# Batch 0's x in 1 KB rows of four tokens, loaded ahead of the weights, with the hand-written order redealt

## The chip, the cores and the metric

The kernel runs on one core of a Trainium2 chip. The core has a matrix engine (TensorE, PE in the profile, with its weight loads listed apart as PEld), a vector engine (VectorE, DVE), a scalar engine (ScalarE, ACT), a general engine (GpSimd, POOL) and a queue engine (SyncE, SP) that mostly issues DMA transfers. ACT can issue DMA transfers too. The metric is the device time of one execution in microseconds (us), the median of several runs.

## The reference

Two stages follow each other. The first reads between tokens and states for each batch and head; the second is a feed-forward network with SwiGLU over all tokens and states.

```
B, H, S, Ns, D = (8, 8, 512, 32, 64)
scores = x @ state.T / sqrt(D);   a  = softmax(scores, over states)
xread  = a @ state                                   # (B, H, 512, 64)
scores2 = state @ x.T / sqrt(D);  a2 = softmax(scores2, over tokens)
sread  = a2 @ x                                      # (B, H, 32, 64)
x = concat([xread, sread], axis=2) -> (8 * 544, 512) # heads side by side
xn  = x / sqrt(mean(x * x) + 1e-6) * rms_g
g   = xn @ w_gate                                    # 512 -> 1536
out = (g * sigmoid(g) * (xn @ w_val)) @ w_out        # 1536 -> 512
```

All arithmetic is float32. The three weight matrices come as float64 in memory and are decoded on the chip.

## The kernel before

**Work and stages.** The 4352 rows are handled as eight batches of 512 tokens, and the 256 states together as a ninth batch. The weights come in 18 pieces of 1 MB of raw float64, gate, val and out for each of six pairs `mp` of 128-column blocks. Four raw buffers exist (`RAW_AHEAD`), so the load of piece k+4 is issued when piece k is decoded. Decoding a piece takes three ACT steps (`exponents`, L223: L237, L239, L242) and four DVE steps (`values`, L246: L263, L266, L270, L275). Only piece 0 (gate of mp 0) is handled in two halves, as two DMAs of 512 KB and two sets of steps. Batch 0 is computed with plain matrix products while the pieces are decoded: `own_weights` (L602) multiplies states with weights (matmuls L615, ACT copies L627), `hidden` (L647) has the matmuls L658, the ACT silu L664 and the DVE product L668, and `project_as_ready` (L858) has the matmuls L865. Batches 1 to 7 use schemes with seven products instead of eight: `hidden_seven` (L752, matmuls L762, ACT copies L814, DVE sums L825 and L838) and `project_twice` (L1034, matmuls L1065, ACT copies L1075, POOL sums L1091, DVE sums L1105, L1115 and L1124).

**The reads.** `tokens_read(b)` (L428) calls `scores` (L305). There, for batches 0 and 1, the states are transposed on PE (L310) and copied to `stT` by DVE (L313); batch 0 also forms products of the states with themselves (L321, `gram` L325). x is transposed by PE in 16 blocks of 128x128 (L333), in four groups through a PSUM tile that ACT copies to `xT` (L335). The score matmuls (L360) give two full tiles of 128x512, one for the even heads and one for the odd. For batch 0, ACT copies both to `sS` (L370), and PE transposes them back so that tokens lie in the partitions (L374, into the PSUM pool named `pv`). Then comes the softmax over states on DVE and ACT: maximum L439, subtraction L441, exponential L443, sum L451, reciprocal L454, product L456. For batch 0 the result is transposed on PE (L464) and copied to `aT_s` by ACT (L467), the squares are summed (L477, L480, L391, L396), GpSimd takes the power −1/2 (L292), four transpositions lay it along the rows (L299), and DVE multiplies it in (L500). The first L658 needs L500. For later batches the tokens' read itself is a matmul (L486), which waits for DVE's transposition L459. `states_read(b)` (L504) takes the softmax over tokens from `sS` (maximum L513, exponential L520); from batch 2 on, the exponentials go to DRAM and back with another layout (store L541, four loads L545, issued by ACT), then come the matmuls L556, the DVE scaling L567 and a transposition L571.

**How x is loaded.** For batches from 2 on, `load_x` (L128) lays token 4p+c in partition p at place c: one DMA of 1 MB, in which each partition and head gets four neighbouring tokens, 1 KB in one piece. For batches 0 and 1, token 128c+p lies in partition p: four DMAs of 256 KB, each in pieces of 256 B (one token of one head). For batch 0 two of these are issued by ACT and two by SP. SP's loads at the start stand in this order: first half of piece 0, the four DMAs of the states of batch 0 (L126), SP's part of x, second half of piece 0, piece 1, `rms_g`, pieces 2 and 3, states and x of batch 1.

```
    halves = load_parts(0)
    next(halves, None)
    load_state(0)
    load_x(0, nc.scalar, nc.scalar, nc.sync, nc.sync)
    for _ in halves:
        pass
    load_piece(1)
```

**What sets the order.** Each part of the work is a Python generator, a stream with a letter. Strings written by hand name the stream whose next step is emitted, and this order is what each engine's queue gets: an engine runs its own queue in order and waits where another engine's result is missing. `ORDER` deals the start and batch 0 (letters: `a` and `s` the token and state reads of batch 0, `A` and `S` those of batch 1, `e` exponents, `d` values, `v` own weights, `h`, `t`, `u` the three parts of `hidden`, `p`, `c` the projection, `w`, `k` preparations for batch 1, and `z` `keep_awake` at L1192, one 128x256 matmul (L1197) on the identity that nothing reads). `FIRST` deals batch 1 together with the reads of batch 2, `PERIOD` batches 2 to 6, `LAST` batch 7, and `STATES` the ninth. In these, `h`, `t`, `u` are the products, silu and sums of `hidden_seven`, `p`, `c`, `k` those of `project_twice`, `a` and `s` the reads of the next batch, `q` quarter sums of weights, `f`, `g`, `l` fetches and loads that SP issues, and `o` stores.

**Buffers in PSUM** around the change: pool `aps` ("at") has two tiles, `vps` ("pv") two, `fx` two, `fy` and `fz` one each, and each is one bank of 128x512 float32.

Of the kernel before, what the change touches and what calls it, by code (L numbers as in the profile page):

```python
# [8 lines left out]
F32 = mybir.dt.float32  # L9
# [8 lines left out]
P = 128  # L18
# [1 line left out]
W_BUFS = 3  # L20

ORDER = (
    "ddzzzzzzzzzezzzeezaaaaaaaaaaaaddaezddaseaaazzaeaaazzdaaaazdeezzzazzaaaazeeaaaadd"
    "aaadaaeAdadsdeezezAdavaaAvAAAAvhehteeAeAdddduhhppdAddtdeeedvvvudeeedphhdtheeddtA"
    "ddddeupdAAAdhAdedeeuedppvpsdAvvddAedhhpetudeeeddhtsAAdhudpAeppdddeAAeedddvAdsvvA"
    "eedphhtuseessseedddeeAhtsdhesppsdvdupdvvdhheeAddAdAtsshtpAudApAedpdhededdveuAApA"
    "AAvvheAdAtSAASSeSSdphSddShAtASuShAkuSSwwpwwkcpSScpSkkckpkcwkkkkkwwwwk"
)

PERIOD = (  # L30
# [4 lines left out]
)  # L35

FIRST = (
    "vhththhhthfhhuuuhtttuqqqqaxxaaauhthhhvquuhuxqxxaavtuhhththhfaxthhhqqquuuuxxtuhut"
    "hthhthhuaakaavfuuxhtuuhutthqqfhhutxxuqqqqqqhauthuuxhhaautthaaasshtuuhuuthuGhskuk"
    "GuGukkppqqpppqpppugqqpkkkklkppqpppkcpcqgaakppgqqkskaakaaaaqqppkkpppkppkkpkpkpkpa"  # L40
    "cosaaaacgpapgaskkkkkkaosaapppppgcppppcaappaskkakkapppkpapkappaakpookkoosaassfsww"
    "xssswxlscxxcoxofxg"
)
LAST = (
    "vxhhffththhtuhhhavuttuuhhtfuhhgxxthhhuuuxxtuthuhtthuhuxhutuvxxxvhthhutkxghhtuhut"
# [11 lines left out]
def kernel(  # L57
# [61 lines left out]
    x_sb = {}  # L119
# [6 lines left out]
            nc.sync.dma_start(out=rows[b][Ns * j:Ns * j + Ns], in_=src)  # L126

    def load_x(b, *queues):  # L128
        if b > 1:
            x_sb[b] = one.tile([P, H, NC, D], F32, name="x_b")  # L130
            nc.sync.dma_start(out=x_sb[b].rearrange("p h c d -> p h (c d)"),
                              in_=x[b].rearrange("h (p c) d -> p h (c d)", c=NC))
            return
        x_sb[b] = (one if b else x_0).tile([P, NC, H * D], F32, name="x_b")
        for c in range(NC):
            (queues or (nc.sync,))[c % max(1, len(queues))].dma_start(
                out=x_sb[b][:, c].rearrange("p (h d) -> p h d", h=H),
                in_=x[b, :, P * c:P * c + P, :].rearrange("h p d -> p h d"))

# [165 lines left out]
    def scores(b, packed, soft):  # L305

        xb = x_sb[b]
        stT = one.tile([P, 4, Ns], F32, name="stT")
        tp = aps.tile([P, 4, Ns], F32, name="at")
        TE.transpose(out=tp.rearrange("p j n -> p (j n)"),  # L310
                     in_=packed.rearrange("p e d -> p (e d)"), identity=ident)
        yield
        VE.tensor_copy(stT, tp)  # L313
        yield "step"
# [12 lines left out]

        if b < 2:
            xT = one.tile([P, 4, NC, P], F32, name="xT", tag="xT")
            for c in range(NC):  # L330
                tp = aps.tile([P, 4, P], F32, name="at")
                for j in range(4):
                    TE.transpose(out=tp[:, j, :], in_=xb[:, c, P * j:P * j + P], identity=ident)  # L333
# [23 lines left out]
        sp = [aps.tile([P, S], F32, name="at") for e in range(2)]  # L357
        for j in range(4):
            for e in range(2):
                TE.matmul(out=sp[e][Ns * j:Ns * j + Ns, :], lhsT=stT[D * e:D * e + D, j, :],  # L360
                          rhs=xT[D * e:D * e + D, j],
                          start=True, stop=True)
        yield


        sS = read[b] = (one if b else x_0).tile([P, 2, NC, P], F32, name="sS")
        eS = one.tile([P, 2, S // Ns, Ns], F32, name="eS", tag="eS")
        soft.update(st=stT, e=eS, raw=[eS[:, e] for e in range(2)])
        for e in range(2) if b == 0 else ():
            SE.copy(sS[:, e].rearrange("p c t -> p (c t)"), sp[e])  # L370
            yield
            tp = vps.tile([P, NC, P], F32, name="pv")
            for c in range(NC):
                TE.transpose(out=tp[:, c, :], in_=sS[:, e, c, :], identity=ident)  # L374
# [53 lines left out]
    def tokens_read(b):  # L428
# [21 lines left out]
        for e in range(2):  # L450
            VE.reduce_sum(out=z1[:, e], in_=eS[:, e], axis=AXX)  # L451
            yield
            VE.tensor_scalar(z1[:, e], z1[:, e], 1e-9, None, op0=ALU.add)
            VE.reciprocal(z1[:, e], z1[:, e])  # L454
            yield
            VE.tensor_tensor(out=eS[:, e], in0=eS[:, e], in1=along(z1, e), op=ALU.mult)  # L456
            yield
            if b:
                VE.transpose(out=aT_s[b][:, e], in_=eS[:, e].rearrange("p k n -> p (k n)"))  # L459
                yield "step"  # L460
                continue
            tp = aps.tile([P, NC, P], F32, name="at")
            for c in range(NC):
                TE.transpose(out=tp[:, c, :], identity=ident,  # L464
                             in_=eS[:, e, 4 * c:4 * c + 4].rearrange("p j n -> p (j n)"))
            yield
            SE.copy(aT_s[b][:, e], tp.rearrange("p c t -> p (c t)"))  # L467
            yield "step"


# [33 lines left out]
    def states_read(b):  # L504
# [47 lines left out]
        for e in range(2):  # L552
            for c in range(NC):
                for j in range(4):
                    h = 2 * j + e
                    TE.matmul(out=rp[Ns * j:Ns * j + Ns, e, :],  # L556
                              lhsT=(e2T[:, j, e, c, :] if b > 1 else
                                    flat[:, e, c, Ns * j:Ns * j + Ns]),
                              rhs=(xb[:, h, c, :] if b > 1 else xb[:, c, D * h:D * h + D]),
                              start=(c == 0), stop=(c == NC - 1))  # L560
        if b == 1:
            load_state(2)
# [650 lines left out]

    parts_0, banks_0 = {}, []
    halves = load_parts(0)
    next(halves, None)
    load_state(0)
    load_x(0, nc.scalar, nc.scalar, nc.sync, nc.sync)
    for _ in halves:
        pass  # L1220
    load_piece(1)
# [79 lines left out]
```

## Time and profile before

| | us |
|---|---|
| median of 3 runs (lowest, highest) | 760.69 (760.42, 761.26) |
| the profiled execution | 759.33 |
| its span, from first to last instruction | 757.5 |
| PE busy in the span | 743.8 (98%) |
| DVE busy | 599.3 (79%) |
| ACT busy | 350.1 (46%) |
| POOL busy | 295.2 (39%) |
| first DVE step of batch 0's softmax (L439) | 16.34 |
| first matmul of batch 0's FFN (L658) | 33.82 |

The profile describes one execution. Its times count from the start of the span, and line numbers are those of the kernel before; the changed kernel has other line numbers for the same statements. A group row names a line, an engine, an operation and its tiles, then its count, busy time and mean length, and what the engine waited for ahead of it. A row of waits gives the total, the number and the longest of the waits of one line for another. The chain of work that ended last is followed back from the end, at each step to what released it. Matmul starts follow each other faster than the length of one row says, since matmuls overlap.

### The profile page before, as it was taken

What the parts mean: (1) busy time and instruction counts of PE and PEld (TensorE: products, weight loads), DVE (VectorE), ACT (ScalarE), POOL (GpSimd) and SP (SyncE); (2) the same over time, 40 slices, a digit from 0 to 9 for tenths busy, and PEclk for the clock granted to TensorE, in tenths of its full rate; (3) what the DMA queues carried; (4) which work ended last, traced back from release to release, by engine and by line L of the source; (5) the groups of instructions that cost most, each with busy time, mean ns of one, the idle gap of its engine ahead of it and who ended that gap; (6) DMA issues with size and microseconds to landing.
All of it is one profiled execution on the core that took longest, in us unless ns stands there. A gap on an engine that the chain in (4) does not pass through costs nothing.

```text
span 757.5 us, 14370 instructions
## 1 busy us (share of the span) xinstructions
PE 743.8 (98%) x5618; PEld 592.5 (78%) x5618; DVE 599.3 (79%) x998; ACT 350.1 (46%) x546; POOL 295.2 (39%) x379
## 2 busy tenths in 40 slices
PE   8899999999899999999999999999999999999998
PEld 6534434678777898879877997789788987899997
DVE  3999996779957897689948994799579965787961
ACT  4889965544235522653255425543455236411220
POOL 3000003892584326542474129312843266323600
PEclk9999999999999999999999999999999999999999
DMA  9887855695576276825784377617661765132311
GB/s 283 234 296 249 315 185 184 243 306 168 188 238 229 45 272 215 292 58 191 248 279 118 143 258 239 195 58 303 217 225 30 302 206 214 55 100 111 139 56 29
DMA packets 61891, 146.17 MB, mean 193 GB/s; under 512 B 15744, under 2 KB 32640, under 8 KB 54912
## 3 DMA queue, kind: packets, MB, share of 16 engines
q1 hardware_dynamic: 48704, 125.78, 47.6%
q10 hardware_dynamic: 13120, 19.47, 9.0%
q8 instruction: 45, 0.74, 0.4%
q14 instruction: 22, 0.18, 0.1%
HBM read 116.46 MB, written 28.77 MB: 192 GB/s over the span
## 4 chain that ended last, share of the span: by engine, by line
PE 91%; DVE 7%; issue 1%; ACT 1%; POOL 0%; DVEq 0%; POOLq 0%
PE f L762 37%; PE f L1065 28%; PE f L865 6%; PE pv L658 6%; PE at L615 3%; PE pv L615 3%; PE f L928 2%; PE f L1197 1%; PE at L556 1%; PE at L360 1%; PE at L486 1%; DVE hb L1124 1%; PE at L299 0%; DVE hb L838 0%; DVE eS L456 0%
## 5 line engine op out<-in xcount | busy, mean ns | idle before, releaser
L762 PE MATMUL f<-aT_s,v 128*128 128x256 f32 x504 | 119.6, 382 | 0.0
L762 PEld LDWEIGHTS f<-aT_s,v 128*128 128x128 f32 x504 | 94.5, 190 | 24.8 <-issue 8.4
L1091 POOL TENSOR_TENSOR kept<-kept 128x256 f32<-128x256 f32 x28 | 23.1, 824 | 174.9 <-DVE kept L1105 173.8
L825 DVE TENSOR_TENSOR g<-g,f 128x512 f32<-128x512 f32 x84 | 57.3, 686 | 39.4 <-PE f L762 35.4
L1075 ACT COPY kept<-f 128x512 f32<-128x512 f32 (+1 forms) x56 | 29.6, 532 | 124.8 <-PE f L1065 83.1
L762 PE MATMUL f<-aT_t,vs 128*128 128x256 f32 x336 | 87.1, 383 | 0.0
L1065 PE MATMUL f<-w,h 128*128 128x128 f32 x588 | 74.6, 276 | 1.0 <-DVE h L1115 1.0
L762 PEld LDWEIGHTS f<-aT_t,vs 128*128 128x128 f32 x336 | 62.5, 190 | 15.3 <-POOL vs L642 4.2
L1065 PEld LDWEIGHTS f<-w,h 128*128 128x128 f32 x588 | 69.6, 192 | 5.5 <-issue 4.1
L816 ACT ACTIVATE hb<-g 128x1024 f32<-128x1024 f32 x42 | 44.4, 1057 | 56.6 <-DVE g L825 56.5
L642 POOL TENSOR_TENSOR vs<-v 128x256 f32<-128x256 f32 x42 | 31.4, 748 | 79.5 <-ACT v L627 79.5
L292 POOL TENSOR_TENSOR ri<-ss,mhalf 128x4 f32<-128x4 f32 x8 | 10.7, 1341 | 117.4 <-DVE ss L396 107.5
L814 ACT COPY g<-f 128x512 f32<-128x512 f32 x42 | 24.6, 586 | 45.0 <-PE f L762 45.0
L762 PE MATMUL f<-aT_t,v 128*128 128x256 f32 x168 | 43.5, 381 | 1.6 <-DVE c L825 1.6
L865 PE MATMUL f<-wo,hb 128*128 128x512 f32 x96 | 44.8, 603 | 0.0
L658 PE MATMUL pv<-aT_s,v 128*128 128x512 f32 x96 | 43.9, 595 | 0.1
L762 PE MATMUL f<-aT_s,vs 128*128 128x256 f32 x168 | 43.6, 382 | 0.0
L838 DVE TENSOR_TENSOR hb<-hb,c 128x512 f32<-128x512 f32 (+1 forms) x48 | 36.7, 764 | 8.0 <-ACT hb L816 7.2
L838 DVE TENSOR_TENSOR hb<-hb,f 128x512 f32<-128x512 f32 (+1 forms) x48 | 31.0, 646 | 15.0 <-PE f L762 14.8
L1065 PE MATMUL f<-wo,h 128*128 128x128 f32 x336 | 42.2, 275 | 0.0
L1065 PE MATMUL f<-wo,hb 128*128 128x128 f32 x336 | 42.1, 275 | 0.0
L825 DVE TENSOR_TENSOR c<-c,f 128x512 f32<-128x512 f32 (+1 forms) x48 | 31.2, 651 | 12.6 <-PE f L762 12.5
(206 smaller groups left out, 1681.4 us busy)
## 6 DMA issues: line engine op xcount, KB each, us to landing
w_m<-w_d SPq DMA_DIRECT2D x48, 1024.0 KB, 6.0
w<-t_d SPq DMA_DIRECT2D x49, 576.0 KB, 5.3
out_dram<-kept SPq DMA_DIRECT2D x56, 128.0 KB, 1.8
raw<-in_moe_w_val_dram SPq DMA_DIRECT2D x6, 1024.0 KB, 5.8
raw<-in_moe_w_out_dram SPq DMA_DIRECT2D x6, 1024.0 KB, 8.5
w_d<-w_m SPq DMA_DIRECT2D x6, 1024.0 KB, 4.9
x_b<-in_x_dram SPq DMA_DIRECT2D x6, 1024.0 KB, 7.6
x_d<-xB ACTq DMA_DIRECT2D x6, 1024.0 KB, 4.2
```

The costliest lines, as they stand in the source:

```text
L615: TE.matmul(out=pv[e][Ns * j:Ns * j + Ns, :], lhsT=stT_g[b][D * e:D * e + D, j, :], rhs=w[D * e:D * e + D, j].rearrange("p m k f -> p (m k ...
L642: GE.tensor_tensor(out=vs[:, 0], in0=a21, in1=a22, op=ALU.add)
L658: TE.matmul(out=to[0], lhsT=lhs(i, k), rhs=r, start=(i == 0), stop=(i == len(rhs) - 1))
L762: TE.matmul(out=ps[:, i, 0:half], lhsT=l[:, i, :], rhs=r, start=(start and i == 0 and k == 0), stop=(k == len(lhs) - 1), skip_group_check= ...
L814: SE.copy(gates(q)[1], q["x"][:, :, 0:half])
L816: SE.activation(out=hb[:, 2 * mp:2 * mp + 2, 0:n].rearrange("p m (c t) -> p m c t", c=2), in_=q["g"][:, :, :, 0:half], func=ACTF.Silu if s ...
L825: VE.tensor_tensor(out=to, in0=to, in1=q[ps][:, :, 0:half], op=ALU.add)
L838: VE.tensor_tensor(out=part, in0=part, in1=val, op=ALU.mult)
L865: TE.matmul(out=banks[r], lhsT=hb[:, m, P * r:P * r + P], rhs=wo[:, m, :], start=(m == 0), stop=(m == NM - 1))
L1065: TE.matmul(out=to[half][:, slot, :], lhsT=lhs[:, k, :], rhs=rhs[:, k, :], start=(fresh and n in (0, 4) and k == 0), stop=(k == QM - 1), s ...
L1075: SE.copy(k[:, 4 * i:4 * i + 4 - i], banks[name][i])
L1091: GE.tensor_tensor(out=k[:, 1:3], in0=k[:, 0:1].to_broadcast([P, 2, QD]), in1=k[:, 1:3], op=ALU.add)
```

## The change

- `load_x` gives batch 0 the layout of the later batches, token 4p+c in partition p. It is loaded by two DMAs of 512 KB in 1 KB pieces: heads 0 to 3 on ACT's queue, heads 4 to 7 on SP's.
- The states and x of batch 0 are issued ahead of both halves of piece 0.
- In `scores` for batch 0, each of the 16 transpositions takes two places (c, c+1) of one head, so that a transposed block holds one token place in the lower 64 partitions and the next in the upper 64. For this, the states are needed on both halves for every head: DVE copies the two heads of a pair in exchanged order to `swapped`, PE transposes this as well, and DVE copies both results to `both` (128x256).
- The score matmuls of batch 0 become 16 of 256 columns into four half tiles (two "at", two "pv"), ACT's copies to `sS` become four of 256 columns, and the transpositions back go to a tile of `fx`.
- The copy to `aT_s` puts the tokens back into their natural order, and the state read of batch 0 takes x by head and place.
- `ORDER` and `FIRST` are dealt anew. Four keep-awake matmuls stand ahead of the first real one on PE where there were thirteen rows of it before (26 matmuls of the record). Behind L500 on DVE stands the third step (L270) of piece 2, which stood ahead of it. In batch 1, PE's L486 stands later and its L556 and L571 earlier; `PERIOD`, `LAST` and `STATES` are as they were.

```diff
     def load_x(b, *queues):
+        if b == 0:
+            x_sb[b] = x_0.tile([P, H, NC, D], F32, name="x_b")
+            n = H // len(queues)
+            for k, queue in enumerate(queues):
+                heads = slice(n * k, n * k + n)
+                queue.dma_start(out=x_sb[b][:, heads].rearrange("p h c d -> p h (c d)"),
+                                in_=x[b, heads].rearrange("h (p c) d -> p h (c d)", c=NC))
+            return
...
     def scores(b, packed, soft):
...
+        if b == 0:
+            swapped = x_0.tile([P, 2, D], F32, name="swapped")
+            for e in range(2):
+                VE.tensor_copy(swapped[:, e], packed[:, 1 - e])
+            yield
+            both = x_0.tile([P, 2, 4, Ns], F32, name="both")
+            tp = aps.tile([P, 2, 4, Ns], F32, name="at")
+            for k, rows_ in enumerate((packed, swapped)):
+                TE.transpose(out=tp[:, k].rearrange("p j n -> p (j n)"),
+                             in_=rows_.rearrange("p e d -> p (e d)"), identity=ident)
+            yield
+            VE.tensor_copy(both, tp)
+            stT = both[:, 0]
+            yield "step"
...
+        if b == 0:
+            xT = one.tile([P, 4, 4, P], F32, name="xT", tag="xT")
+            for j in range(4):
+                tp = aps.tile([P, 4, P], F32, name="at")
+                for k in range(4):
+                    TE.transpose(out=tp[:, k, :], identity=ident,
+                                 in_=xb[:, 2 * j + k // 2, 2 * (k % 2):2 * (k % 2) + 2].rearrange("p c d -> p (c d)"))
+                yield
+                SE.copy(xT[:, j], tp)
+                yield "step"
...
+        if b == 0:
+            halves = [[pool.tile([P, 2 * P], F32, name=name) for e in range(2)]
+                      for pool, name in ((aps, "at"), (vps, "pv"))]
             for e in range(2):
-                TE.matmul(out=sp[e][Ns * j:Ns * j + Ns, :], lhsT=stT[D * e:D * e + D, j, :],
-                          rhs=xT[D * e:D * e + D, j],
-                          start=True, stop=True)
+                for j in range(4):
+                    for i in range(2):
+                        here = slice(D * i, D * i + D)
+                        TE.matmul(out=halves[i][e][Ns * j:Ns * j + Ns, :], lhsT=both[here, (e + i) % 2, j, :],
+                                  rhs=xT[here, j, 2 * e:2 * e + 2], start=True, stop=True)
...
         for e in range(2) if b == 0 else ():
-            SE.copy(sS[:, e].rearrange("p c t -> p (c t)"), sp[e])
-            yield
-            tp = vps.tile([P, NC, P], F32, name="pv")
+            for i in range(2):
+                SE.copy(sS[:, e, i::2], halves[i][e].rearrange("p (k t) -> p k t", k=2))
+            yield
+            tp = fx.tile([P, NC, P], F32, name="f")
...
-            SE.copy(aT_s[b][:, e], tp.rearrange("p c t -> p (c t)"))
+            SE.copy(aT_s[b][:, e].rearrange("p (t c) -> p t c", c=NC), tp.rearrange("p c t -> p t c"))
...
-                              rhs=(xb[:, h, c, :] if b > 1 else xb[:, c, D * h:D * h + D]),
+                              rhs=(xb[:, h, c, :] if b != 1 else xb[:, c, D * h:D * h + D]),
...
     halves = load_parts(0)
+    load_state(0)
+    load_x(0, nc.scalar, nc.sync)
     next(halves, None)
-    load_state(0)
-    load_x(0, nc.scalar, nc.scalar, nc.sync, nc.sync)
     for _ in halves:
         pass
     load_piece(1)
```

The two strings, cut (each letter one step):

```diff
 ORDER = (
-    "ddzzzzzzzzzezzzeezaaaaaaaaaaaaddaezddaseaaazzaeaaazzdaaaazdeezzzazzaaaazeeaaaadd"
...
+    "zzzzaaaaaaaaaaaaaaddeaaesaaaaedeazzzzzazdaaaaeedazzzzzedeaaaazzdadeezzaaaaddaadA"
+    "eeeaAadvvAvaaadeesdAAahthAAhddddehtupeeddduAAAdsdpedepveddpvvdddedeedhthAhhuddAe"
...
 FIRST = (
-    "vhththhhthfhhuuuhtttuqqqqaxxaaauhthhhvquuhuxqxxaavtuhhththhfaxthhhqqquuuuxxtuhut"
-    "hthhthhuaakaavfuuxhtuuhutthqqfhhutxxuqqqqqqhauthuuxhhaautthaaasshtuuhuuthuGhskuk"
...
+    "vxhhthhthhthuxuufththaaaaaqfhhqthahtqqquuuuxavvhuhhxxtuthuhthtuhuhuaqhvfxxxtuqqqx"
+    "tqhqqqqhutkqqhqtaahauhuGGhutuhhhutGuuhtthhhxxuuxtqqquaaauaahhhthagthhthsuuuuuuhp"
...
```

More of the change, by code (lines that the diff above doesn't have):

```diff
@@ L22 @@
 ORDER = (
-    "ddzzzzzzzzzezzzeezaaaaaaaaaaaaddaezddaseaaazzaeaaazzdaaaazdeezzzazzaaaazeeaaaadd"
[L24 to L27, printed above, removed]
+    "zzzzaaaaaaaaaaaaaaddeaaesaaaaedeazzzzzazdaaaaeedazzzzzedeaaaazzdadeezzaaaaddaadA"
+    "eeeaAadvvAvaaadeesdAAahthAAhddddehtupeeddduAAAdsdpedepveddpvvdddedeedhthAhhuddAe"
+    "edppedAAeeAtddveeupvvhhheddtddAepeeedtAAdhsuddpsdudAddedeedppeevpvvhAAddAdAedsht"
+    "uddedsseeAsedshhdtuppvevvphhApdAedteeeeAdeAdshduepAdtAdAAsdApAAddddehueevvAASSAv"
+    "pShSSAAAptddSSSSdSdhhAuhkkAtuwSwskSSkkkwpcSwpcpcskkpcwwkkkwwkw"
 )
@@ L37 @@
 FIRST = (
-    "vhththhhthfhhuuuhtttuqqqqaxxaaauhthhhvquuhuxqxxaavtuhhththhfaxthhhqqquuuuxxtuhut"
-    "hthhthhuaakaavfuuxhtuuhutthqqfhhutxxuqqqqqqhauthuuxhhaautthaaasshtuuhuuthuGhskuk"
-    "GuGukkppqqpppqpppugqqpkkkklkppqpppkcpcqgaakppgqqkskaakaaaaqqppkkpppkppkkpkpkpkpa"
-    "cosaaaacgpapgaskkkkkkaosaapppppgcppppcaappaskkakkapppkpapkappaakpookkoosaassfsww"
-    "xssswxlscxxcoxofxg"
+    "vxhthhthhthuxuufththaaaaaqfhhqthahtqqquuuuxavvhuhhxxtuthuhthtuhuhuaqhvfxxxtuqqqx"
+    "tqhqqqqhutkqqhqtaahauhuGGhutuhhhutGuuhtthhhxxuuxtqqquaaauaahhhthagthhthsuuuuuuhp"
+    "ppkpptukupuqqqqkkppukkkkkppaakkkggkcacppppppppcappppssaaakplqapkkkkkpkkkppppaaak"
+    "ccaasapppssakscfqaaaapqkkappkkkakppppakkosasqksappppskssgglsaoooapspppakkkaooafw"
+    "wxsxxpgcpcowxoxfxg"
 )
@@ L133, in load_x @@
             return
-        x_sb[b] = (one if b else x_0).tile([P, NC, H * D], F32, name="x_b")
+        x_sb[b] = one.tile([P, NC, H * D], F32, name="x_b")
         for c in range(NC):
-            (queues or (nc.sync,))[c % max(1, len(queues))].dma_start(
+            nc.sync.dma_start(
                 out=x_sb[b][:, c].rearrange("p (h d) -> p h d", h=H),
@@ L307, in scores @@
         xb = x_sb[b]
[L308 to L311, printed above, removed]
-        yield
-        VE.tensor_copy(stT, tp)
-        yield "step"
+        if b == 0:
[12 more added lines that the diff above has]
+            yield "step"
+        else:
+            stT = one.tile([P, 4, Ns], F32, name="stT")
+            tp = aps.tile([P, 4, Ns], F32, name="at")
+            TE.transpose(out=tp.rearrange("p j n -> p (j n)"),
+                         in_=packed.rearrange("p e d -> p (e d)"), identity=ident)
+            yield
+            VE.tensor_copy(stT, tp)
+            yield "step"
         if b == 0:
@@ L326, in scores @@
             yield "step"
-        if b < 2:
+        if b == 0:
[7 more added lines that the diff above has]
+                SE.copy(xT[:, j], tp)
+                yield "step"
+        elif b == 1:
             xT = one.tile([P, 4, NC, P], F32, name="xT", tag="xT")
@@ L354, in scores @@
             xT = xT.rearrange("p g j r -> p j g r")
-        sp = [aps.tile([P, S], F32, name="at") for e in range(2)]
-        for j in range(4):
+        if b == 0:
+            halves = [[pool.tile([P, 2 * P], F32, name=name) for e in range(2)]
+                      for pool, name in ((aps, "at"), (vps, "pv"))]
             for e in range(2):
-                TE.matmul(out=sp[e][Ns * j:Ns * j + Ns, :], lhsT=stT[D * e:D * e + D, j, :],
-                          rhs=xT[D * e:D * e + D, j],
-                          start=True, stop=True)
+                for j in range(4):
[3 more added lines that the diff above has]
+                                  rhs=xT[here, j, 2 * e:2 * e + 2], start=True, stop=True)
+        else:
+            sp = [aps.tile([P, S], F32, name="at") for e in range(2)]
+            for j in range(4):
+                for e in range(2):
+                    TE.matmul(out=sp[e][Ns * j:Ns * j + Ns, :], lhsT=stT[D * e:D * e + D, j, :],
+                              rhs=xT[D * e:D * e + D, j],
+                              start=True, stop=True)
         yield
```

## The prediction

> **What bounds the kernel now.** I read the page first. TensorE (PE) is busy 98% of the span and carries 91% of the chain that ended last; VectorE (DVE) has the next 7%.
>
> ```profile
> PE 743.8 (98%) x5618; PEld 592.5 (78%) x5618; DVE 599.3 (79%) x998; ACT 350.1 (46%) x546; POOL 295.2 (39%) x379
> PE 91%; DVE 7%; issue 1%; ACT 1%; POOL 0%; DVEq 0%; POOLq 0%
> ```
>
> So time can be won only where PE isn't doing work that the result needs: in the start, and in its waits. Second view, the table by stretches (busy time of PE, PE weight loads, DVE, ACT, POOL; then clock, DMA share, GB/s). The cuts are mine: 33.82 is the first L658, where PE starts the FFN of batch 0; 134.37 is about where batch 1 starts.
>
> ```profile
> 0.00:30.27 30.27, 25.16 (x152) 17.75 (x152) 18.44 (x34) 18.18 (x24) 6.44 (x28) 1.00 0.96 250
> 33.82:134.37 100.55, 100.55 (x515) 42.97 (x515) 92.19 (x120) 80.21 (x101) 7.50 (x9) 1.00 0.71 249
> 134.37:757.50 623.13, 614.90 (x4921) 529.85 (x4920) 485.16 (x841) 248.39 (x418) 280.57 (x342) 1.00 0.53 181
> ```
>
> From 33.82 to 134.37 PE never idles, though DVE is 92% busy beside it. The 25.16 us of PE in the start are mostly keep-awake matmuls (L1197), which compute nothing. Third view, the chain in order of time (start, length, what):
>
> ```profile
> 1.46 8.50 PE f L1197 x26
> 9.96 0.12 PE at L310
> ...
> 10.75 0.60 PE at L333 x4
> ...
> 13.83 1.20 PE at L360 x16
> ...
> 16.34 0.70 DVE m L439
> ...
> 30.70 1.13 DVE raw L266
> ...
> 33.17 0.61 DVE aT_s L500
> 33.77 0.04 issue
> 33.82 0.70 PE pv L658
> ```
>
> Until 9.8 nothing real has run on PE. Then come transposition, scores and softmax; from 16.34 to 33.77 the chain is DVE alone, without a gap that counts: softmax of batch 0 mixed with the decoding of three and a half weight pieces. So the start has two limits: when the state and x land, and then the sum of DVE's work. Fourth view, the same table for two short stretches: while the 2 KB pieces of the first half of gate move, and while x moves in 256 B pieces.
>
> ```profile
> 3.20:4.00 0.80, 0.80 (x3) 0.62 (x3) 0.00 (x0) 0.00 (x0) 0.80 (x5) 1.00 1.09 383
> 6.00:8.00 2.00, 2.00 (x9) 1.69 (x8) 0.21 (x1) 1.17 (x2) 0.32 (x1) 1.00 1.35 211
> ```
>
> Last column: 383 GB/s against 211. Fifth view, PE's waits from 134 to 230, which is batch 1 (total, times, longest):
>
> ```profile
> PE f L762 <- DVE c L825: 1.6, 1, 1.6
> PE at L486 <- DVE aT_s L459: 1.0, 1, 1.0
> PE f L1065 <- DVE h L1115: 1.0, 1, 1.0
> PE at L571 <- DVE sr L567: 0.7, 1, 0.7
> ```
>
> That is 4.3 us, all that FIRST can win. The rows of L545 in that stretch say when the exponentials of batch 2's state read come back from DRAM:
>
> ```profile
> DMA to landing us min/median/max: 5.3/7.4/7.5
> ```
>
> [...] the 128x256 keep-awake matmuls take 634 ns until about 6 us and 379 after.
>
> **The change, part by part.**
>
> *Landing.* Before: first half of gate (512 KB) at 4.96, rows and x behind it, rows usable at about 9.5. After: rows (64 KB) and x (1 MB) lead, gate follows. Bytes start to flow at about 2 us. At 383 GB/s the 1.06 MB are in by 4.8, at 211 by 7.0. Pieces of 1 KB are nowhere in this trace; [...] the rows' 256 B pieces share the engines, so I take 300: x complete at about 5.6 to 6.3, rows at 4.75, first half of gate 1.4 us later (7.7; bounds 6.3 and 8.4).
>
> *To the first L439.* Two DVE copies (128x64), two transpositions instead of one, one 128x256 copy instead of 128x128 (0.30 us, so about 0.45): the gram matmuls at about 6.15, x's transpositions from 6.6. Their 16 with four copies took 10.75 to 13.83, 3.1 us; the same again, so score matmuls at 9.7. From there to L439 it was 16.34 − 13.83 = 2.5: now 16 matmuls of 256 columns for 8 of 512 (nothing to +0.2), and ACT's four copies of 256 columns for two of 512 (about 0.35 against 0.58 each, +0.13), while the four early transpositions no longer wait for a "pv" bank. So L439 at 12.3. Only 4 keep-awake matmuls stand ahead instead of 13, then PE waits for the rows: if it is cold in the transpositions (0.17 us apart, 634/379 times that is 0.28), 16 x 0.11 = 1.8 more, of which the ACT copies (4 x 0.585) hide some. I take 12.65, bounds 12.3 and 14.1.
>
> *DVE from L439 to L658.* Before: L439 at 16.34, L500 at 33.08: 16.74. The decoding of the first half of gate was done ahead of L439 (DVE waited 5.0 for that landing and 3.9 for L310); now its last two steps (L270 and L275, 0.60 each) and the first two of the second half (0.40 and 0.60) come behind: +2.2. The L270 of the third piece (1.13) is dealt behind L500. Sum 17.8, less a 0.28 issue gap that has no reason to recur, 17.5; bounds 17.5 and 18.1, since L270 now waits for ACT's third step (about 13.8 to 14.5), and the reciprocal root on POOL (1.40, then L299) has only 2.3 us of DVE work over it instead of 3.6, against 2.6 that the path needs. I take 17.85. L658 follows L500's start by 0.74: 12.65 + 17.85 + 0.74 = 31.25, against 33.82: **2.6 us won**, from 1.0 (14.1 and 18.1) to 3.3.
>
> *33.8 to 134.* Four x transpositions of batch 1 that stood ahead of L658 stand behind it: 4 x 0.11 = +0.44 on a full PE. DVE has 1.13 more to do here: 92.2 becomes 93.3 beside 101. The pieces decoded are due at L615; queue against queue, each is done 0.3 to 1 us ahead of it. That cover is thin; gone, the excess is paid once, at most about 1. I take nothing. Start, net: **−2.2**.
>
> *FIRST.* PE's read of batch 2 (L486) stands 1.34 us later against DVE's L459 only 0.5 later: wait 1.0 to about 0.1. L571 stands further behind L567: 0.7 to nothing. One L513 less ahead of L825: 1.6 to about 0.7. L1115 slightly better (−0.3). Sum −2.8. Against it: L556 stands 5.6 us of PE work earlier, while its slack after the last L545 landing (217.0) was 0.6 (it began at 217.63). The loads are issued earlier too: I put their landing at 211 to 213, against PE's arrival at about 210.2, so with the semaphore a new wait of 1 to 3, taken 2.1; behind it stands PE's whole queue. Net **−0.7**, from −1.8 to +0.2. SP's fetches move among themselves with weights a period ahead, and POOL's L1091 sums only interleave: POOL has 174.9 us of idle ahead of them, cost nothing; if a bank's store were late it would show as a wait for L1091.
>
> *The rest.* The permuted read of the aT_s copy: 0 to +0.6 each of two, hidden by DVE's decoding between. PERIOD, LAST and STATES are unchanged, 0.
>
> Sum: −2.2 − 0.7 = −2.9. The profiled execution took 759.33 (span 757.5 and 1.83 around it): 756.4. The median shown is 760.69, 1.36 more; the same distance gives **757.7**.
>
> **The rivals**, on the median's scale.
> - More: PE is warm, x lands by 5, L556 finds its data. −3.3 + 0.4 − 1.8 = −4.7: **756.0**. The keep-awake row argues against a warm PE.
> - Eaten: x lands at 7.0 and PE is cold: L439 at 14.1 gives −1.0 + 0.44 = −0.6; with FIRST at −0.2, **759.9**. For it: both transfers share the same engines, and DVE, not landing, sets 17 of the 31 us.
> - Slower: L556. If its loads land when they did, at 217.0, PE waits until 217.2 with the 5.6 us of matmuls that used to fill this time now behind it: every other gain upstream is absorbed, and batch 1 loses 217.2 + 5.6 − 217.63 − 0.7 = 4.5. With the start's −2.2 that is +2.3: **763.0**. It decides from a loss of 3.7 on, i.e. if the loads come less than 0.8 us earlier than before. For it: landings of 7.4 us there against a median of 3.4 over all batches. Against: the new order moves the store and loads forward on ACT too.
> - The change doesn't do what it says, because DVE alone sets L658: excluded in part, since L439 itself moves; it is the "eaten" case.
>
> **Chances.** About 0.2%, 1.5 us, is what a measurement of this kernel can tell from no change. Forecast (756.0 to 759.2) 0.58; more 0.07; eaten 0.20; slower 0.15. Faster is the first two, 0.65; same 0.20; slower 0.15. The range leaves out the slower case and a little of "more": 755.3 to 760.8.
>
> **What would show it.** First L439 between 12 and 14 and first L658 near 31.2; x's packets at 300 GB/s or more; no wait of PE in the 100 us after L658; in batch 1 no wait at L486 or L571, and one at L556 of 1 to 3. Wrong if L658 comes after 32.5, if L615 waits for DVE's w_m, or if L556's wait exceeds 3.

## The result: no difference that can be measured

The changed kernel takes 760.96 us (median of 21 runs, 757.65 to 764.07) beside 760.39 for the kernel before (21 runs, 759.11 to 761.63): a ratio of 1.0006, 95% interval [0.9995, 1.0017]. The forecast was 757.7. Its runs spread over 6.4 us where those of before spread over 2.5, and they go with the clock that the throttle granted to TensorE, averaged over the run (1.000 is full speed): at 0.998 the two runs took 757.65 and 758.30, at 0.993 the eight runs took 762.0 in the median. A straight line through the 21 runs loses 0.67 us for each 0.001 of clock (correlation −0.75) and, drawn on beyond the runs, reaches 757.4 at a clock of 1.000. An estimate for comparison: 0.001 of a span of 758 us is 0.76 us of full-speed work, so most of the clock that is lost goes with a longer run.

The profiled execution took 760.29 (span 758.5). First the two lines of its page on engines and on the chain that ended last:

```profile
PE 745.1 (98%) x5619; PEld 592.8 (78%) x5619; DVE 599.4 (79%) x1000; ACT 349.8 (46%) x548; POOL 294.9 (39%) x379
PE 87%; DVE 6%; ACT 2%; DMA 2%; issue 1%; POOL 1%; SPq 0%; ACTq 0%; DVEq 0%
```

PE has 1.3 us more of busy time, though fewer keep-awake matmuls run (38 in the record, 54 before); and DMA has 2% and POOL 1% of the chain, where POOL had 0% before and DMA had no part. The table by stretches, cut at the first L702 (L658 before) and at the first matmul of batch 1:

```profile
0.00:32.88 32.88, 28.52 (x181) 19.18 (x182) 20.73 (x40) 20.88 (x30) 6.36 (x28) 0.91 0.88 268
32.88:134.66 101.78, 101.61 (x519) 43.56 (x519) 96.47 (x123) 80.39 (x102) 9.22 (x9) 0.99 0.69 245
134.66:758.50 623.84, 614.97 (x4928) 530.06 (x4920) 482.17 (x838) 248.55 (x418) 279.35 (x342) 1.00 0.53 180
```

Before, batch 1 began at 134.30. So the start became 0.94 shorter (forecast 2.6), the next stretch 1.30 longer (forecast 0.44), the rest 0.64 longer (forecast 0.7 shorter). In the rest, batch 1 took 0.3 less, batch 4 took 0.7 more, and the end, from the last long run of matmuls on, took 0.3 more. The third number from the end, the clock, is 0.91 in the start; before it was 1.00. Two views show where. The chain in order of time (start, length, what):

```profile
5.52 0.83 PE at L324 x2
...
7.21 2.85 PE at L356 x12
...
13.27 0.62 DVE m L483
...
26.74 1.49 PE f L435 x8
28.23 1.89 PE f L659 x16
30.11 1.04 PE at L366 x4
31.16 0.85 PE pv L307 x4
32.01 0.85 PE at L366 x4
...
32.88 3.37 PE pv L702 x6
```

and the stretches around its lower half (third number from the end: clock):

```profile
24.00:26.00 2.00, 1.76 (x19) 0.80 (x15) 1.97 (x3) 1.97 (x3) 0.00 (x0) 1.00 1.00 362
26.00:28.00 2.00, 1.74 (x13) 1.65 (x12) 2.00 (x4) 0.55 (x1) 0.00 (x0) 0.79 0.27 96
28.00:30.00 2.00, 2.00 (x18) 0.36 (x17) 1.75 (x5) 1.18 (x1) 1.40 (x1) 0.50 0.66 265
30.00:32.00 2.00, 2.00 (x17) 1.96 (x10) 0.75 (x1) 1.80 (x3) 0.00 (x0) 0.50 1.04 266
32.00:34.00 2.00, 1.98 (x7) 1.09 (x6) 1.95 (x3) 1.95 (x4) 0.00 (x0) 0.50 0.91 367
34.00:36.00 2.00, 2.00 (x6) 0.89 (x5) 1.97 (x3) 1.85 (x3) 0.00 (x0) 1.00 0.39 158
```

From about 27 to 34 PE has half its clock; such a stretch is called a dip below. Before, DVE carried the chain from 16.3 to 33.8; now it loses it at 26.7 to a PE whose matmuls take about twice as long: L659's sixteen 1.89 us instead of 1.02, a group of four transpositions 0.85 to 1.04 instead of about 0.5. What goes ahead in the trace is a stretch of 5 us (23.1 to 28.2) with narrow matmuls, L521 on 32 rows and L435 with one column, and a single transposition of 128x128. The last keep-awake matmuls end at 22.2. The clock falls at 27.18 and stays low for 6.83 us; in the 2.00 us ahead of the fall PE is busy for 1.74.

In batch 1, PE's waits from 134 to 230 (total, times, longest):

```profile
PE at L600 <- DMA e<-e_d: 1.5, 1, 1.5
PE f L806 <- ACT g L853: 1.2, 2, 0.8
PE f L1109 <- DVE h L1159: 0.9, 1, 0.9
PE f L806 <- DVE c L869: 0.8, 1, 0.8
PE f L1109 <- DVE h L1161: 0.4, 1, 0.4
```

The waits at the tokens' read and at the last transposition are gone and the one for L825 is halved, as forecast; L600 (L556 before) waits for its loads, as forecast, and two new small waits appeared. In sum 4.8 us instead of 4.3. (Not every wait is time lost: batch 1 as a whole still took 0.3 less.)

A third loss, 0.7 us, lies in batch 4, whose order is unchanged. The first of these rows, from the profile after, and the second, from that before, give the time that the four loads of transposed x took from issue to landing there:

```profile
DMA to landing us min/median/max: 3.3/5.0/6.0
```

```profile
DMA to landing us min/median/max: 3.4/4.7/5.3
```

The slowest of the four takes 0.7 longer after a like issue time, and the score matmuls of that batch (L403, L360 before) take 1.85 us instead of 1.17:

```profile
411.94 1.85 PE L403 MATMUL at<-xG,stT 64*32 64x512 f32 x16
```

```profile
411.88 1.17 PE L360 MATMUL at<-xG,stT 64*32 64x512 f32 x16
```

Between 404 and 412, after has one transfer more, of instructions; before has only the second of these rows there:

```profile
q8 instruction: 1, 0.02, 1.0%
q14 instruction: 1, 0.01, 0.2%
```

### The profile page after: what moved, and what is told of

Read it like the earlier page. It is cut to its first block, busy times and chain, and to the rows that moved or that the text cites. A ratio compares the mean times of both kernels' runs of the same rounds, so it can differ in the third digit from the quotient of the medians.

```text
span 758.5 us, 14372 instructions
## 1 busy us (share of the span) xinstructions
PE 745.1 (98%) x5619; PEld 592.8 (78%) x5619; DVE 599.4 (79%) x1000; ACT 349.8 (46%) x548; POOL 294.9 (39%) x379
## 4 chain that ended last, share of the span: by engine, by line
PE 87%; DVE 6%; ACT 2%; DMA 2%; issue 1%; POOL 1%; SPq 0%; ACTq 0%; DVEq 0%
PE f L806 38%; PE f L1109 26%; PE pv L702 5%; PE f L909 4%; PE at L659 3%; PE pv L659 2%; PE f L972 2%; PE at L600 1%; PE at L403 1%; PE at L530 1%; DMA e<-e_d 1%; DMA out_dram<-kept 1%; DVE hb L1168 0%; DVE hb L882 0%; ACT ex L247 0%
## 5 line engine op out<-in xcount | busy, mean ns | idle before, releaser
L1135 POOL TENSOR_TENSOR kept<-kept 128x256 f32<-128x256 f32 x28 | 23.1, 825 | 176.1 <-DVE kept L1149 174.9
L702 PE MATMUL pv<-aT_s,v 128*128 128x512 f32 x96 | 44.6, 603 | 0.2 <-ACT v L671 0.2
L869 DVE TENSOR_TENSOR c<-c,f 128x512 f32<-128x512 f32 (+1 forms) x48 | 31.3, 652 | 13.7 <-PE f L806 13.7
```

Of the source, the lines that this page charges most:

```text
L702: TE.matmul(out=to[0], lhsT=lhs(i, k), rhs=r, start=(i == 0), stop=(i == len(rhs) - 1))
L869: VE.tensor_tensor(out=to, in0=to, in1=q[ps][:, :, 0:half], op=ALU.add)
L1135: GE.tensor_tensor(out=k[:, 1:3], in0=k[:, 0:1].to_broadcast([P, 2, QD]), in1=k[:, 1:3], op=ALU.add)
```

## The experiments

Theory 1 when they began: the start's gain is real, and is lost to the clock dip at 27. Rival 2: it is lost in batch 1 to the new FIRST. Rival 3: the dip is a whim that no order changes. Each kernel was timed beside the kernel before. Ratios are to the kernel before, with 95% intervals; they aren't quotients of the two medians, which can differ from them by some 0.001. Where the text says so many us faster or slower, it compares medians. Single letters in the strings are steps (`z` a keep-awake matmul, `a` the token read of batch 0, `s` a state read). Line numbers of experiments on the changed kernel are its own: L600 is L556 before, L702 is L658, L356 is L333, L483 is L439.

**Three later keep-awake matmuls** (e1_awake), in the changed kernel:

```diff
 ORDER
-    ...zzaaaaddaadAeeeaAadvv...
+    ...zzaaaazddaazdAeeeaAazdvv...
```

> The changed kernel with three more keep-awake matmuls, behind each of the two gram products L521 and behind L435, where its profile has no full-size matmul from 23.1 to 28.2. Theory 1 (PE falls back to half clock at about 27 because these 5 us hold only narrow matmuls, and this eats the start's gain): granted clock 1.00 over the whole span, first L702 at 31.2 to 31.6 instead of 32.88, about 758.5 with the kernel before at 760.4. Rival 2 (the gain is lost in batch 1 by the new order FIRST): about 761, whatever the clock. Rival 3 (the dip is a whim of the throttle that no order changes): clock still 0.993 to 0.998, about 761.

Measured 761.59 (13 runs), 1.0006 [0.9994, 1.0019]. The start did as theory 1 said: no dip at 27, first L483 at 11.99, first L702 at 30.41. But the time did not. The waits of PE from 190 to 230, and the table around them:

```profile
PE at L600 <- DMA e<-e_d: 3.7, 1, 3.7
PE f L1109 <- DVE h L1159: 0.9, 1, 0.9
PE f L1109 <- DVE h L1161: 0.4, 1, 0.4
```

```profile
206.00:208.00 2.00, 1.79 (x17) 1.59 (x15) 2.00 (x5) 0.00 (x0) 1.84 (x4) 1.00 0.68 210
208.00:210.00 2.00, 0.00 (x0) 0.00 (x0) 1.97 (x4) 0.00 (x0) 1.92 (x2) 1.00 0.77 305
210.00:212.00 2.00, 0.47 (x20) 0.50 (x24) 0.14 (x1) 0.00 (x0) 0.00 (x0) 0.60 0.30 118
212.00:214.00 2.00, 2.00 (x59) 1.83 (x52) 0.47 (x2) 0.00 (x0) 0.00 (x0) 0.50 0.03 8
214.00:216.00 2.00, 2.00 (x11) 2.00 (x11) 1.78 (x7) 0.00 (x0) 1.13 (x1) 0.50 0.43 93
216.00:218.00 2.00, 2.00 (x14) 2.00 (x14) 0.56 (x2) 0.00 (x0) 1.84 (x4) 0.69 0.91 280
```

PE came to L600 near 207.8 and waited 3.7 us for loads of which the slowest took 7.5; a dip of its own came in this wait, from 210 to 217. So theory 1 was half the story, and rival 2 the other half.

**The new FIRST, taken away and added.** In the second kernel (e2_old_first) the changed kernel has the string FIRST of before; in the third (e3_new_first) the kernel before has that of the changed one. No other line differs.

> The changed kernel with the string FIRST of before, all else as changed. Theory 1 (clock): within 0.5 of the changed kernel, 761.3, since FIRST is worth about 0.3 in the profiles (batch 1 took 93.40 before and 93.11 after). Rival 2 (FIRST eats the start's gain): 758.5.

Measured 760.53 (22 runs), 0.9993 [0.9983, 1.0004]: between the two expectations. In its profile the second half of x landed at 9.2 (8.4 in the changed kernel), PE waited 1.2 for it, and dips lie from about 9 to 12 and from about 29 to 33. So the dip in the start is there without the new FIRST too.

> The kernel before with the string FIRST of the changed one, all else as before. Theory 1: 0.3 faster than before, at 760.1. Rival 2: 2 slower, at 762.4.

Measured 763.71 (20 runs), 1.0033 [1.0022, 1.0044]: 3.3 slower, against theory 1 as it stood. Its profile has a wait of 2.8 at L556 and a dip from about 215 to 218, beside one from about 30 to 34; eleven of its 20 runs had a clock of 0.993. The first 30 us are dealt as in the kernel before, whose own profile had no dip there.

**Two keep-awake matmuls fewer in the kernel before** (e4_before_two_less):

```diff
 ORDER
-    ...adsdeezezAdav...
+    ...adsdeeeAdav...
```

> The kernel before without the two keep-awake matmuls between L310 and L615 (at 29.3 to 30.3), so that its stretch of narrow matmuls lasts from 24.6 to 30.3 instead of 29.3. Theory 1: in most runs the clock dips to half there, mean clock 0.995 or so, L658 up to 2 us later, 761.5 to 762.5. Rival 3 (order doesn't matter to the throttle): clock 1.00 and 760.4, since DVE sets L658.

Measured 759.42 (21 runs), 0.9986 [0.9979, 0.9993]: faster, where theory 1 said slower. The dip came (half clock from about 31 to 34, and none of the 21 runs had a clock over 0.998, where 52 of 201 runs of the kernel before had), so here the clock did change with the order, against rival 3. Why the runs are faster all the same isn't shown: in the profiled execution, which took 759.92, L658 comes at 34.46, 0.6 later than before. A microsecond of matmuls that stood ahead of L615 is gone, but that this is the reason was only argued.

**Later keep-awake and the old FIRST** (e5_awake_old_first): the edits of e1 and e2 together.

> The changed kernel with the three more keep-awake matmuls of the first experiment and the string FIRST of before. Theory 1a (two losses eat the start's gain: the clock dip at 27, and in batch 1 PE's wait at L556 for the exponentials' round trip, with a dip behind it; FIRST of before has no such wait): first L702 at about 30.4 against 33.82, less 0.44 of moved transpositions, so 3.0 faster than before, 757.4; no wait of PE for DMA in batch 1, clock 1.00 in most runs. Rival (the loads land by DMA alone at about 211 to 217, so PE, coming 3 earlier, waits for them in any order): a wait of about 2.4 at L600, 759.8.

Measured 759.20 (20 runs), 0.9980 [0.9970, 0.9989]; no wait for DMA in batch 1 and a clock of 1.00 in 11 runs, so theory 1a holds in kind, with 1.2 of the 3.0 us. The profiled execution, at 759.57, shows one loss: L702 at 32.1, since x's transpositions (L356) took 3.76 us here and 2.5 in e1, though the same instructions stand up to there. First e5, then e1 (start, length):

```profile
7.25 3.76 PE L356 MATMUL at<-ident,x_b 128*128 128x128 f32 x16
```

```profile
6.89 1.09 PE L356 MATMUL at<-ident,x_b 128*128 128x128 f32 x8
8.23 1.14 PE L356 MATMUL at<-ident,x_b 128*128 128x128 f32 x8 [0.24 <-ACT xT L359]
```

In e5 the 16 take 3.76 us in one row, in e1 two rows of eight 1.09 and 1.14, while the granted clock of both starts is printed as 1.00. A start with the short rows (2.5 us in all) is called warm below, one with 3.4 to 3.8 us cold. A second loss in this profile lies in batch 4, where L403 took 2.13 us instead of 1.17. The eleven runs with a clock of 1.00 fall into two groups, five at 757.5 to 757.9, near the 757.4 that theory 1a expected, and six at 759.2 to 759.6, the profiled one among them. The profile has 1.65 us from the cold start and 1.0 from batch 4; which of them parts the groups isn't shown.

**Only L556 and L571 back in their old place** (e6_awake_late_states), with e1's matmuls. The edit of FIRST moves the last four steps `s` and the load `l` of x that hangs on them:

```diff
 FIRST
-    ...ppppskssgglsaoooapspppakkkaooafwwxsxxpg...
+    ...ppppsksggaoooappppakkkaooafwwxssxslsxpg...
```

> The changed kernel with the three keep-awake matmuls and the new FIRST, in which only the steps of L556 and L571 (with x's load behind them) are moved back to their old place behind the first own-weight products, some 4.5 us of PE work later. Theory 1a: the wait of 3.7 at L556 and the dip at 210 to 217 are gone, the rest of FIRST's gains stay: 756.8, at or just under the kernel with the old FIRST. Rival (other moves in FIRST cost, such as POOL's or SP's): 759 or more, with L556's wait gone all the same.

Measured 760.57 (14 runs), 1.0002 [0.9990, 1.0013]: a miss. The profiled execution, at 758.55 the fastest of its runs, is nearer what was expected: no wait at L600, L702 at 30.3. The median isn't: with no wait left at L600 it is where the rival put it, and the runs spread from 758.55 to 763.58.

**The loads alone.** e7_before_x_first is the kernel before with states and x issued first; e8_awake_gate_first is e5 with the first half of gate issued first again.

```diff
     halves = load_parts(0)
-    next(halves, None)
     load_state(0)
     load_x(0, nc.scalar, nc.scalar, nc.sync, nc.sync)
+    next(halves, None)
```

> The kernel before with states and x issued ahead of the first half of gate, still in 256 B pieces, nothing else. Theory: x complete near 7, but gate's first half lands at about 8.5, and DVE's first two steps in the old order decode it ahead of the copy of the states, so that copy begins near 9.6 instead of 10.11: 0.3 to 0.5 faster, 760.0. Rival (the landing alone sets the start): L439 3 earlier, 758.

Measured 762.49 (22 runs), 1.0029 [1.0018, 1.0040]. Gate's first half came at 9.81, and DVE, whose old order decodes it first, copied the states only at 10.89; PE stood for 1.4 us and fell to half clock from about 13 to 16.5. Both expectations missed: loads reordered without a redealt DVE cost 2 us. The profiled execution (764.55) has a second dip, from 204 to 208, so how much of the 2 us is the start's isn't shown.

> As the kernel with three keep-awake matmuls and the old FIRST, but with the first half of gate issued ahead of the states and x again (x in 1 KB rows on the two queues, pairs, order as changed). Theory: the states and SP's half of x land about 1.3 later (0.52 MB at 0.38 MB a us), L439 as much later, 758.6. Rival (DVE's work alone sets L702, whenever x lands): 757.4.

Measured 761.17 (21 runs), 1.0012 [1.0004, 1.0020]. PE waited 2.3 for the states (L324 at 7.56), then fell to half clock from about 9 to 12, so that the transpositions of x took 3.58, and L702 came at 33.6. Both expectations were too fast. Against e5 the load order is worth 2.0, more than the 1.2 expected; DVE's work alone doesn't set L702.

**One early keep-awake matmul more.** e9_early_late_states is e6, and e10_early_old_first is e5, each with one `z` between the transpositions of the states and the gram products, where PE waited 0.5 us:

```diff
 ORDER
-    zzzzaaaaaa...
+    zzzzaazaaaa...
```

> The kernel with three later keep-awake matmuls and L556/L571 back in their old place, and one more keep-awake matmul between the transpositions of the states (L310) and the gram products (L321), where PE waits 0.5 for DVE's copy. Theory (in the profiles of the changed kernel and of the one with the old FIRST the transpositions of x took 3.4 to 3.8 at half clock, and in two others 2.4[...]): x's transpositions take 2.4 in nearly every run, L439 at 12.0 to 12.3, median 758.3. Rival (the added matmul only delays the gram products, the start's clock is not what spreads the runs): 760.6, as without it.

> The same four added keep-awake matmuls with the string FIRST of before. Theory: the start's gain as in the other, batch 1 as before: 758.3 (without the early matmul 759.2). Rival: 759.2 or more.

Measured 758.55 (8 runs), 0.9974 [0.9964, 0.9984], and 758.86 (11 runs), 0.9975 [0.9966, 0.9985]: both beat the kernel before by about 2 us, and the changed one too. The first is near what was expected, the second lies between its two expectations. In both profiles the transpositions took 2.5 us, L702 came at 30.6 and 30.5, and the only dip lies after 755, behind the last matmul.

**The late place of L556 without any keep-awake.** e11_before_late_states is the kernel before with the FIRST of e6; e12_late_states is the changed kernel with it.

> The kernel before with the new FIRST, in which only L556 and L571 stand in their old place. With the whole new FIRST it took 763.7. Theory (of FIRST, only the earlier L556 costs, by its wait for the exponentials' round trip and the clock dip behind that): 760.0, at or just under before, no dip near 212. Rival (other moves in FIRST cost): 762 or more.

Measured 760.23 (13 runs), 1.0006 [0.9995, 1.0017], where the whole new FIRST took 763.71: of all that FIRST moves, the early L556, with the load of x that hangs on it, costs 3.5 us; its profile has no dip in batch 1. The rest of FIRST gives nothing that can be measured either: a wait of 1.4 for a quarter of the weights (`w<-t_d`) appears in its profile.

> The changed kernel with only L556 and L571 moved back, no keep-awake matmul added. Theory: the wait and the dip of batch 1 are gone, the cold start and the dip at 27 stay: 759.8, between the changed kernel (761.0) and before. Rival (the dip at 27 and the wait are one loss, paid once): 761.

Measured 760.46 (14 runs, 757.74 to 765.00), 1.0005 [0.9992, 1.0019]. The median lies between the two expectations. The profile caught a run without the two dips, though it has no keep-awake matmul more than the changed kernel; up to batch 1 the two have the same instructions and differ only from run to run. PE in order of time (start, length, what):

```profile
27.25 1.09 PE L659 MATMUL f<-w_m,stT_g 64*32 64x512 f32 x16 [0.28 <-DVE w_m L283]
28.27 0.65 PE L366 MATMUL at<-ident,x_b 128*128 128x128 f32 x4
28.80 0.65 PE L307 MATMUL pv<-ident,ri 128*128 128x128 f32 x4
29.29 0.60 PE L366 MATMUL at<-ident,x_b 128*128 128x128 f32 x4
30.34 3.67 PE L702 MATMUL pv<-aT_s,v 128*128 128x512 f32 x8 [0.45 <-DVE aT_s L544]
```

L702 waits for DVE again, as forecast, and comes at 30.34. The last long run of matmuls starts at 738.29 instead of 741.13: 2.84 earlier. Yet this execution, the fastest of its kernel, took 757.74, only 1.59 less than the profiled one of before: the last two stores took 2.8 us from issue to landing instead of 1.7. (They took 3.2 to 3.4 in the profiles of e6, e10 and e13, whose matmuls also end early; why isn't shown.) Its clock of 0.998 comes from a dip from 753.3 on, behind the last matmul, which costs nothing. The other 13 runs have clocks down to 0.992, and times up to 765.0.

**How the loss divides** (e13_early_only is e12 with the early matmul alone, e14_four_new_first the changed kernel with all four and its own FIRST).

> The changed kernel with L556 and L571 moved back and only the early keep-awake matmul (between the transpositions of the states and the gram products), without the three later ones. Theory (two dips, one at the start and one at 27, each paid): 759.5, between 760.5 (none added) and 758.6 (all four). Rival A (the cold start alone spreads the runs): 758.6. Rival B (only the dip at 27 counts): 760.5.

Measured 760.64 (22 runs), 0.9993 [0.9982, 1.0003], as rival B had it; transpositions 2.5, a dip from about 26.4 to 29.8, L702 at 31.2.

> The changed kernel with all four keep-awake matmuls and its own new FIRST. Theory (the whole start's gain goes into a longer wait at L556, with a clock dip behind it): 761.5, no better than the changed kernel, L702 at 30.5 in the profile and a wait of 3 to 4 at L600. Rival (the start's gain carries through): 758.6, as with L556 in its old place.

Measured 760.49 (14 runs), 0.9991 [0.9977, 1.0004], between the two expectations; a wait of 3.2 at L600 and a dip from about 212 to 216. Its transpositions took 3.76 in spite of the early matmul, and L702 came at 32.1, so one matmul doesn't make the start warm every time.

With L556 late, the four cases are 760.46 (none added), 760.64 (early), 760.57 (three later), 758.55 (all four). Each alone gave nothing and both gave 2 us. That isn't the sum that two separate losses would give; with runs that spread over 2.4 to 7.3 us and 8 to 22 of them each, the division between the start and the dip at 27 stays open.

**When a dip comes.** By the clock of the short stretches, every dip that ends before the last matmul, twelve in nine profiles, lasts about 3.4 us (3.36 to 3.44), or 6.8 in the changed kernel and in e1. In the three profiles with two dips, they begin 20.5 us apart (e2), 184.3 (e3) and 191.1 (e7), which is about 6, 54 and 56 times 3.413, the 54th part of 184.3. Whether changes of the clock always lie such multiples apart isn't shown by three distances. Counted back in steps of 3.413 from its dip (an estimate from these numbers), the changed kernel has a point at 10.1, where x's transpositions went from 421 ns (start at 9.63) to 273 (10.20), and e14 one between 10.6 and 11.2, when nearly all of them had been slow (3.76 us, 7.30 to 11.06); e1 and e13 have one at 5.6 and 5.9, ahead of them (2.5 us). The changed kernel and e2 have the same instructions up to batch 1, but by the same estimate points at 6.7 and at 5.4, so the same instructions met them at different places. So rival 3 was right in part: a clock over 0.998 came in none of 21 runs of e4 and in 52 of 201 of the kernel before, and between the profiles of the changed kernel and of e12, with the same instructions up to batch 1, only the first has the dip at 27.

## Why the prediction was wrong

- *What bounds the kernel: right. The landing: wrong for half of x.* x was to be complete at 5.6 to 6.3; ACT's half landed at 4.9, SP's at 8.4, though DMA made 344 GB/s from 6 to 8, over the 300 assumed (the author's estimate for pieces of 1 KB, between the 211 and 383 measured in the kernel before). The states took until 5.4 instead of 4.75. SP's half is issued at 2.6, behind the states, and shares the engines with gate's, which the working had put behind x: by 8.4, 1.79 MB had moved, where states and x are 1.11. (The working counted 1.06; with 1.11 its bounds are 4.9 and 7.3. It also held that the trace before has no pieces of 1 KB, but the six loads of x for the later batches consist of them.) PE needs that half at about 9, so it cost nothing here; in e2, where it came at 9.2, it did.
- *To the first L439: right in kind.* 12.65 was taken from bounds of 12.3 and 14.1. Warm starts (transpositions of x in 2.5 us: e1, e6, e9, e12) gave 11.9 to 12.4, cold ones (3.44 in the changed kernel, 3.76 in e5) 13.3 to 13.7. Which one comes differs from run to run.
- *DVE from L439 to L658: right where DVE sets the end.* 18.59 was forecast with the 0.74 to L658; e12 gave 17.97, e1 18.42. In the changed kernel it was 19.61, and L702 came at 32.88, past the 32.5 that the prediction had named as a sign of being wrong. **This is the step that failed:** it checked POOL's power and the transpositions behind it against DVE's work, but at PE's full clock. With PE at half clock from 27 on, L435, L659 and twelve transpositions became the chain. (The three and a half weight pieces that the prediction reads into DVE's chain are about two; its sum goes by the single steps and doesn't use this. Its least gain, 1.0, comes to 0.9 from its own terms.)
- *33.8 to 134: the 0.44 was right in place;* 0.6 more came from L702's first matmuls at half clock, 0.2 from a wait for v.
- *FIRST: the size of L556's wait was right in one run (1.5, forecast 1 to 3), its price wrong.* The forecast added the start's gain and FIRST's. They are not independent: with the start earlier, L556 waits longer (1.5 with L702 at 32.9; 3.7 at 30.4), and the waits of 2.8 (e3), 3.2 (e14) and 3.7 (e1) each had a dip of 3.4 or 6.8 us with them; the wait of 1.5 had none. In e3 FIRST cost 3.3 where −0.7 was forecast; in the changed kernel's profile batch 1 did take less, by 0.3. **This is the second step that failed.** The mechanism of the "slower" rival exists, but its point of decision, loads less than 0.8 earlier than before, was wrong: in e3 L556 got its data at 214.2, 2.8 ahead of the 217.0 of before, and it still cost.
- *PERIOD "unchanged, 0":* 0.7 in the profile, with a transfer of instructions beside x's loads in batch 4. In twelve of the sixteen profiles L403 (L360) took 1.60 to 2.13 us there, in the other four, those of before, e3, e4 and e12, 1.09 to 1.25. Between 404 and 412 such a transfer (queue 8) is seen in six of the twelve (the changed kernel, e1, e2, e5, e7 and e8) and in none of before, e3 and e4; but e6, with 1.60, has none there either. That the one causes the other was not tried.
- The "eaten" rival named a cold PE, at the start only; it came out at 759.9 and the true median at 761.0, since the dip at 27 and the dip behind L556 were in neither part of its sum.

So the gain forecast for the start is there in the profiles with a warm start and no dip ahead of L702: L702 came at 30.3 to 30.6 in five profiles, where 31.25 was forecast. The whole gain reached the end in no profile: e12, with L556 late, was 2.84 us ahead of before at its last run of matmuls and 1.59 at the end, where 2.9 was forecast for the changed kernel. In the median run of the changed kernel half clock takes the gain back, with batch 4 adding its 0.7 in the profile. That e9 and e10 take 2 us less than the kernel before, with four keep-awake matmuls more and L556 in its old place, shows that the clock and the wait at L556 are what takes it; their shares aren't shown.

## What to carry to other kernels

When a start is shortened, look at what the removed time did for TensorE's clock: keep-awake matmuls and waits belong to the schedule like real work (e9 and e10, with four keep-awake matmuls more, took 758.55 and 758.86, the changed kernel 760.96). Here a stretch of 5 us of narrow matmuls (the changed kernel) and waits of 2.8 to 3.7 us (e3, e14, e1) had dips of 3.4 or 6.8 us at half clock with them or behind them. Move a consumer of a DMA round trip ahead only as far as its data are early in the faster kernel, not in the one that was profiled. And take several runs with their clock before one profile is believed: the profiled execution of e12 and its median differ by 2.7 us.

## What the runs showed of the hardware

- In the changed kernel PE fell to half clock at 27.18, after 2.00 us in which the trace had it busy for 1.74 (87%), mostly with matmuls of 32 rows or one column: there, being busy did not keep the clock up. How little work is too little isn't shown; e12's profile had the same narrow matmuls (23.5 to 27.0) and no dip at that place.
- The twelve dips that end before the last matmul last about 3.4 or 6.8 us. Where a profile has two, they begin 20.5, 184.3 and 191.1 us apart (e2, e3, e7).
- Slow matmuls at the start didn't show in the granted clock: with 1.00 printed, x's 16 transpositions took 2.5 us in e1 and 3.76 in e5, which have the same instructions up to there.
- The kernel before has dips too: of 201 runs of it beside these experiments, only 52 had a mean clock of 0.999 or more. They go with 0.29 us for each 0.001, against 0.67 in the changed kernel. Where they lie isn't known: in the changed kernel PE, and not DVE, is on the chain behind the dip at 27, while dips behind the last matmul, as in e12, lower the mean clock and cost nothing.
